# A list of ranks in place of due times, raw weights in the home of low parts, and other first products in an attention and gated-MLP kernel

## The chip, the cores and the metric

The kernel runs on one core of one Trainium2 chip. The metric is the device time of one launch in microseconds. The core has a matrix engine (PE, with its weight loads shown apart as PEld), three elementwise engines (DVE, ACT, POOL) and a queue engine, SP, that issues the DMAs.

## The reference

Four batches, four heads, 1088 positions, head width 32. Attention uses a feature map of 8 x 8 products instead of a softmax. Its output x (1088 x 128 per batch) goes through a gated MLP whose gate mixes positions with a 1088 x 1088 matrix.

```
a = S1 x ; b = S2 x ; phi(x) = outer(a, b).reshape(64)          # for q and k
kv = sum_s phi(k) v ; z = sum_s phi(k)
x = (phi(q) kv) / (phi(q) z + 1e-6)                             # per batch 1088 x 128
h = relu(x @ w_in) ; u, v = h[..., :512], h[..., 512:]
v_n = (v - mean(v)) / sqrt(var(v) + 1e-6)
v_s = w_spatial @ v_n + b_spatial                               # mixes the positions
out = (u * v_s) @ w_out
```

## The kernel before

All large products are done in split precision. An operand is a rounded high part plus a low part (the difference), and a product is three matrix instructions: high x high, low x high, high x low (`mm3`, `high`, `low`). ACT makes a high part by a cast, DVE or POOL makes the low part by a subtraction.

The spatial matrix W is loaded transposed, in 9 row tiles of 128 (`kt` 0 to 8) and 3 column pieces of 424, 332 and 332 (`c` 0 to 2; the text calls piece c "placement" c). `load_w(kt, c)` loads one raw tile `wt<kt><c>` into one of seven `pl` buffers, casts it into `wTh` and subtracts into `wTl`. The raw buffer is free again when both are done. For the first two pieces the subtraction runs on DVE, for the third on POOL. `wTh` and `wTl` are whole arrays of 9 x 1152 columns. `w_in` and `w_out` arrive as 64-bit numbers and are converted in seven DVE or ACT steps each (`from_f64`, tiles `wi_x1`, `wi_x0`, `wo_x`).

Batch 0 has a form of its own. `attention0` computes the keys' features (`kab`, `kp`), sums them into `kv0`, then per group of 384 positions computes the queries' features, turns them (`tq`), divides (`nd`, `rec`, `x32`), turns back (`xt`) and splits x into `xh` and `xl`; `hidden_v` makes `vt`, its mean and variance (`st`, `mv`, `rs`, `nm`) and normalises it. `main` then issues for batch 0 the products with the high part of W for all four column blocks d (`sp0d0`, kt 0 to 8), after them the products with its low part, then the gates (`u`, `g`) and the output products (`po`). Batches 1 to 3 do the same work in `attention` and `main` while the batch before is still on PE.

Nothing is executed in program order. Each operation is registered with `op` (engine, cost in ns, reads, writes) and a planner, `Order.schedule`, runs a timeline: at each step it takes, for each engine, the operations that could start within a small slack of the earliest one, and of these the one with the lowest `due`; the engine that can start first goes. A due time is worked back from the last operations with the costs, then moved by a table of numbers by name, `LEADS`. For DMAs the planner assumes one stream at 0.38 KB per ns, with 1950 ns until the first byte counts and once 1900 ns extra. The result is one fixed order per engine; on the chip every engine executes its own list in order and waits on semaphores.

Before the first data are there PE multiplies zeros (`N_WARM` products of 128 x 128, tile `wps`), and up to 50 us the planner puts unread products of 64 columns (`Fill`, L471) into gaps of PE that it foresees.

Of the kernel before, what the change touches and what calls it, by code (L numbers as in the profile page):

```python
# [45 lines left out]
}  # L46
DR_BUFS = {"qd": 6}
# [59 lines left out]
class Whole:  # L107


    def __init__(self, k, tag, name, shape, dt=F32):  # L110
# [16 lines left out]
class Fill:


    def __init__(self, fn):  # L130
        self.fn = fn


class Order:


# [73 lines left out]
    def schedule(self):  # L210
        ops = self.ops
        for o in reversed(ops):
            eng, cost, _ = o.alts[0]
            own = max(cost - self.OV[eng], 20) if eng != "PE" else cost + 165
            if eng == "SP":
                own = cost + 2000 + o.kb / 0.39
            own *= o.stretch
            dues = [s.due - own - self.LAT.get((eng, s.eng), 35) for s in o.succ]
            if o.due is not None:
                dues.append(o.due)  # L220
# [1175 lines left out]
```

## Time and profile before

| what | us |
|---|---|
| median of the three runs | 333.25 |
| the three runs | 327.79, 333.25, 333.78 |
| the profiled execution's own time | 326.74 |
| its span, first to last instruction | 325.0 |

The span is 1.74 us shorter than the time of the same execution. In the views, a line such as L978 is a line of the kernel, "sp<-wTl,vh" says what is written from which operands, and x8 how many instructions a row merges. Times are counted from the start of the span. Matrix instructions are pipelined: the duration of one is longer than the step from one to the next, so the text works with steps.

### The profile page before, as it was taken

The numbers are of one execution on the slowest core, as the hardware profiler recorded it, in microseconds if no ns is written. First come the engines' busy times: TensorE is split into PE (matmuls) and PEld (weight loads), VectorE is DVE, ScalarE is ACT, GpSimd is POOL, SyncE is SP. The second block draws the span as 40 slices with busy tenths as digits, with TensorE's granted clock in tenths as the row PEclk, the third lists the DMA queues.
The fourth block names the chain that finished last, engine by engine and source line by source line (L and its number), as shares of the span: only waits on it lengthen the run. The fifth ranks groups of instructions, "written<-read, shape, count | busy, mean of one in ns | idle before, by whom it ended". The sixth has DMA issues, their size and how long they took to land.

```text
span 325.0 us, 6726 instructions
## 1 busy us (share of the span) xinstructions
PE 318.4 (98%) x2580; PEld 303.7 (93%) x2580; DVE 228.6 (70%) x513; ACT 166.1 (51%) x390; POOL 64.6 (20%) x81
## 2 busy tenths in 40 slices
PE   8899999999999999999999999999999999999995
PEld 7787999899999899999899999999999999999995
DVE  4799997646699973789986558897235697429382
ACT  2498667435774634566536457562314465416050
POOL 1000002486101026320103802150001321103000
PEclk9999999999999999999999999999999999999999
DMA  7832168854020274001034206001000321000001
GB/s 216 288 105 87 54 173 272 266 172 131 3 69 20 83 239 162 1 5 45 21 117 137 63 30 185 2 0 37 8 0 2 105 86 42 0 3 0 2 1 69
DMA packets 21548, 26.82 MB, mean 83 GB/s; under 512 B 2828, under 2 KB 21260, under 8 KB 21516
## 3 DMA queue, kind: packets, MB, share of 16 engines
q1 hardware_dynamic: 21516, 26.39, 26.2%
q8 instruction: 20, 0.33, 0.4%
q14 instruction: 12, 0.10, 0.1%
HBM read 23.31 MB, written 3.06 MB: 81 GB/s over the span
## 4 chain that ended last, share of the span: by engine, by line
PE 81%; DVE 8%; DMA 5%; ACT 3%; SPq 2%; issue 1%; ACTq 0%
PE sp L969 16%; PE sp L971 14%; PE sp L978 14%; PE sd L1203 4%; PE sp L1203 3%; PE sd L444 3%; PE sd L445 3%; PE sd L446 3%; PE pu L444 2%; PE po L445 2%; PE po L444 2%; DMA pl<-in_wT 2%; PE po L446 2%; PE sp L980 2%; PE pu L445 2%; PE pu L446 2%
## 5 line engine op out<-in xcount | busy, mean ns | idle before, releaser
L969 PE MATMUL sp<-wTh,vh 128*128 128x332 f32 (+1 forms) x350 | 114.8, 328 | 0.0
L971 PE MATMUL sp<-wTh,vl 128*128 128x332 f32 (+1 forms) x304 | 98.9, 325 | 0.0
L978 PE MATMUL sp<-wTl,vh 128*128 128x332 f32 (+1 forms) x304 | 97.0, 325 | 0.0
L969 PEld LDWEIGHTS sp<-wTh,vh 128*128 128x128 f32 x350 | 65.8, 188 | 2.2 <-issue 1.0
L971 PEld LDWEIGHTS sp<-wTh,vl 128*128 128x128 f32 x304 | 57.1, 188 | 0.6
L978 PEld LDWEIGHTS sp<-wTl,vh 128*128 128x128 f32 x304 | 57.1, 188 | 0.2
L454 DVE TENSOR_TENSOR g<-u,g 128x332 fp32r<-128x332 f32 (+1 forms) x41 | 24.3, 593 | 18.1 <-PE po L445 11.6
L523 ACT CAST g<-u 128x332 fp32r<-128x332 f32 (+1 forms) x41 | 19.8, 490 | 31.9 <-DVE u L1006 21.6
L1006 DVE TENSOR_TENSOR u<-sp,u 128x332 f32<-128x332 f32 (+1 forms) x43 | 22.3, 520 | 19.1 <-PE sp L980 12.6
L779 DVE RECIPROCAL c<-c 128x384 f32<-128x384 f32 (+1 forms) x9 | 21.8, 2419 | 16.0 <-ACT c L777 16.0
L961 ACT ACTIVATE u<-pu 128x332 f32<-128x332 f32 (+1 forms) x44 | 20.6, 469 | 22.0 <-PE pu L446 17.7
L882 ACT CAST vh<-vt 128x384 fp32r<-128x384 f32 x36 | 17.3, 511 | 20.6 <-DVE vt L841 11.6
L805 DVE BATCH_NORM_STATS2 st<-vt 128x6 f32<-128x512 f32 x36 | 24.0, 684 | 2.2 <-ACT vt L803 2.0
L748 POOL TENSOR_TENSOR pl<-pl,pl 128x384 f32<-128x384 f32 (+1 forms) x18 | 17.9, 1004 | 37.4 <-DMA pl<-qd 37.3
L457 POOL TENSOR_TENSOR r<-pl,r 128x384 fp32r<-128x384 f32 (+1 forms) x18 | 17.7, 988 | 36.8 <-ACT r L523 36.8
L803 ACT ACTIVATE vt<-sd 128x512 f32<-128x512 f32 x36 | 21.3, 603 | 7.1 <-PE sd L446 6.3
L884 DVE TENSOR_TENSOR vl<-vt,vh 128x384 fp32r<-128x384 f32 (+1 forms) x36 | 17.8, 505 | 5.3 <-ACT vh L882 5.2
L570 POOL TENSOR_TENSOR wTl<-pl,wTh 128x332 fp32r<-128x332 f32 (+1 forms) x9 | 8.2, 935 | 55.5 <-ACT wTh L567 52.6
L444 PE MATMUL pu<-xh,wih 128*128 128x332 f32 (+1 forms) x48 | 16.5, 344 | 0.4 <-ACT kp L961 0.2
L841 DVE TENSOR_SCALAR vt<-vt,mv,sm 128x512 f32<-128x512 f32 x33 | 16.7, 556 | 0.0
L567 ACT CAST wTh<-pl 128x332 fp32r<-128x332 f32 (+1 forms) x27 | 12.7, 499 | 7.1 <-DMA pl<-in_wT 6.9
L446 PE MATMUL pu<-xh,wil 128*128 128x332 f32 (+1 forms) x48 | 15.8, 329 | 0.0
(279 smaller groups left out, 641.6 us busy)
## 6 DMA issues: line engine op xcount, KB each, us to landing
pl<-in_wT SPq DMA_DIRECT2D x34, 166.0 KB
v<-in_vA SPq DMA_DIRECT2D x12, 198.0 KB
kt<-in_kT SPq DMA_DIRECT2D x12, 192.0 KB
pl<-qd SPq DMA_DIRECT2D x12, 192.0 KB
pl<-qd SPq DMA_DIRECT2D x24, 96.0 KB
pl<-in_wT SPq DMA_DIRECT2D x9, 212.0 KB
c<-in_qT SPq DMA_DIRECT2D x9, 192.0 KB
out<-u SPq DMA_DIRECT2D x6, 166.0 KB
```

The costliest lines, as they stand in the source:

```text
L444: nc.tensor.matmul(o, ah, bh, start=start, stop=False)
L445: nc.tensor.matmul(o, ah, bl, start=False, stop=False)
L446: nc.tensor.matmul(o, al, bh, start=False, stop=stop)
L454: return lambda: nc.vector.tensor_tensor(out=o(), in0=a(), in1=bb(), op=ALU.subtract)
L779: op("DVE", 135 + 6.3 * n, lambda x32=x32, n=n: nc.vector.reciprocal(out=x32[:, :n], in_=x32[:, :n]), w=[x32])
L803: op("ACT", c_act(512, True), lambda pv=pv, t=t: nc.scalar.activation(vt[:, t], pv.ap, AF.Relu), r=[pv], w=[(vt, t)])
L805: op("DVE", 690, lambda stats=stats, t=t: nc.vector.bn_stats(out=stats.ap, in_=vt[:, t]), r=[(vt, t)], w=[stats])
L969: nc.tensor.matmul(sp[:, :cw], vh[:, kt], wTh[:, kt, cs], start=(kt == begin), stop=False)
L971: nc.tensor.matmul(sp[:, :cw], vl[:, kt], wTh[:, kt, cs], start=False, stop=False)
L978: nc.tensor.matmul(sp[:, :cw], vh[:, kt], wTl[:, kt, cs], start=False, stop=False)
L1006: op("DVE", c_dve(cw), lambda: nc.vector.tensor_tensor(out=u.ap, in0=sp[:, :cw], in1=u.ap, op=ALU.mult), r=[sp], w=[u], lead=LEAD[1])
L1203: nc.tensor.matmul(x[:, :cw], p, q, start=i == 0 and n == 0, stop=end and i == 3 and n == 2)
```

## The change

Five things are changed.

- The raw tiles of the first piece of W (kt 0 to 7) no longer use the `pl` buffers. The array `wTl` is cut into `wTl<kt>` (448 columns, piece 0) and `wl<kt>` (704 columns, pieces 1 and 2) at the same places in memory, and raw `wt<kt>0` is loaded into the home of `wl<kt>`, which is written for good only later, by the low parts of pieces 1 and 2.
- PE starts with 5 products of zeros in place of 8, and then issues 28 unread products of 32 x 32 columns at four positions of the array.
- Due times and `LEADS` go. `due` is the place of the operation in a list of 1806 names, `ORDER`; the planner and its slacks stay. (`FIRST` still sets a due time, which is then overwritten by the rank.)
- The planner's DMA model is slower: 0.265 KB per ns in place of 0.38, first byte after 1500 ns, once 500 ns extra. Some PE costs, the switch between 4-byte and rounded products (`TURN`) and the size given for `w_in` are raised.
- Loads get earliest times: 7 us for piece 0 of W, 13 us for pieces 1 and 2; those of batch 1 go from 35 to 24 us.

The computation is the same.

```diff
-N_WARM = 8
+N_WARM = 5
+N_SMALL = 28
...
+SB_BUFS.update((f"wl{kt}", 1) for kt in range(NK))
...
-    (0, "wTh", "wTl", "xh", "xl", "g", "c", "r", "b32"),
+    (0, "wTh", *(f"{x}{kt}" for kt in range(NK) for x in ("wTl", "wl")), f"wTl{NK}", "xh", "xl", "g", "c", "r", "b32"),
...
-FIRST = ()
-AFTER = (0, 35.0, 0, 0)
+FIRST = ("s_raw", "kt00", "kt01", "kt02", "v00", "v01", "v02", "qt00", "ident_sb", "mask_sb", "wi_raw1", "qt01")
+AFTER = (0, 24.0, 0, 0)
+AFTER_W = (7.0, 13.0, 13.0)
...
+ORDER = """
+kt00:1 z9:1 eps:2 z9:2 s_raw:1 eps:1 v92:1 wps:1 v93:1 v00:1 wps:2 v90:1 v91:1 wps:3 kt01:1 wps:4
+qt00:1 wps:5 kt02:1 wps:6 wi_raw1:1 sk:1 sk:2 b32:1 sk:3 sk:4 ident_sb:1 sk:5 sk:6 v01:1 sk:7 v02:1
+kab00:1 kab01:1 qt01:1 ka00:1 kp00:1 ka01:1 mask_sb:1 wt80:1 kp01:1 kab02:1 kv0:1 ka02:1 kp02:1 qab00:1 qa00:1 qp00:1
+wt50:1 wi_x1:1 qt02:1 tq00:1 bh:1 wi_x1:2 tq01:1 wi_raw0:1 qpT00:1 bl:1 kv0:2 wi_x1:3 qpT01:1 wt20:1 wi_x1:4 wt40:1
+kv0:3 wi_x1:5 wTl:11 qab01:1 kd0:1 wi_x1:6 wt00:1 nd00:1 qa01:1 wTh:9 wt10:1 qp01:1 wt01:1 wTh:6 wi_x1:7 tq10:1
+wt11:1 tq11:1 rec0:1 wTl:9 wih:1 qab02:1 rec0:2 wTl:6 qa02:1 x320:1 qpT10:1 qpT11:1 qp02:1 xt0:1 nd01:1 wt30:1
+wi_x0:1 wil:1 xh0:1 wt70:1 wi_x0:2 wTh:3 tq20:1 xl0:1 wt60:1 tq21:1 wTh:5 rec1:1 wi_x0:3 pv000:1 wt21:1 rec1:2
+wi_x0:4 wTh:1 wTl:10 pv001:1 x321:1 vt00:1 wt31:1 wi_x0:5 qpT20:1 xt1:1 st000:1 wt41:1 qpT21:1 pv002:1 xh0:2 wi_x0:6
+wt51:1 vt00:2 nd02:1 xl0:2 wTh:11 wo_raw:1 st001:1 vt00:3 wTh:10 wi_x0:7 wt61:1 pv010:1 wTh:8 mv00:2 rec2:1 wih:2
+st002:1 pv011:1 wTh:7 rec2:2 mv00:1 mv00:3 x322:1 qt10:1 qt11:1 vt01:1 qt12:1 wTl:7 vt01:2 xt2:1 wil:2 sd00:1
+pv012:1 wTh:12 xh0:3 rs00:1 st010:1 wTh:4 pu000:1 xl0:3 vt01:3 t100:1 wTh:2 st011:1 pv020:1 u000:1 t100:2 st012:1
+pv021:1 wTh:13 vt02:1 rs00:2 mv01:1 pu010:1 nm00:1 mv01:3 mv01:2 vt02:2 vt00:4 pv022:1 u010:1 wTl:8 vh00:1 pab10:1
+vt00:5 vt02:3 pu020:1 st020:1 vl00:1 abT10:1 sd01:1 pab11:1 vt00:6 qd10:1 pab12:1 rs01:1 wTl:3 qd10:2 sp000:1 abT11:1
+u020:1 t101:1 wTl:2 sp010:1 qd11:1 vh00:2 pu030:1 t101:2 wTl:1 vh00:3 qd11:2 sp030:1 rs01:2 vl00:2 wTh:15 sp020:1
+wTh:16 nm01:1 st021:1 vl00:3 sp030:2 vt01:4 sp000:2 st022:1 sp010:2 vt01:5 sp020:2 wTl:13 sp020:3 vh00:4 mv02:3 mv02:1
+wt71:1 mv02:2 sp010:3 vt01:6 vh00:5 sp030:3 vl00:4 sd02:1 sp000:3 vh00:6 rs02:1 vl00:5 sp020:4 wo_x:1 sp030:4 t102:1
+abT12:1 vl00:6 sp010:4 wTh:14 qd12:1 sp000:4 t102:2 wo_x:2 wTh:17 sp010:5 qd12:2 rs02:2 wTl:12 sp020:5 nm02:1 wo_x:3
...
+""".split()
...
-TURN = 125
+TURN = 150
...
+RATE, SLOW_AT, SLOW_BY, LATENCY = 0.265, 4000, 500, 1500
...
-            o.due = round((min(dues) if dues else 1e9) - o.lead)
+        rank = {name: n for n, name in enumerate(ORDER)}
+        for o in ops:
+            o.due = rank[o.name]
...
-                dma = max(dma, s + cost + 1950) + o.kb / (0.38 if o.kb > 0 else -0.12)
-
-                if dma > 5000 and not slow:
-                    slow, dma = True, dma + 1900
+                dma = max(dma, s + cost + LATENCY) + o.kb / (RATE if o.kb > 0 else -0.12)
+
+                if dma > SLOW_AT and not slow:
+                    slow, dma = True, dma + SLOW_BY
...
+    def small():
+        for i in range(N_SMALL):
+            q = 32 * (i % 4)
+            nc.tensor.matmul(wps[q:q + 32, :32], z9[:, q:q + 32], z9[:, :32], start=True, stop=True, tile_position=(0, q))
+
+    op("PE", 1000, f4=True, fn=small, r=[z9], w=[wps], due=0)
...
-    wTl = tl(None, "wTl", [P, NS, ROW], F32R)
+    wl_first = [tl(None, f"wTl{kt}", [P, WIDE], F32R) for kt in range(NK)]
+    wl_last = tl(None, f"wTl{NK}", [P, ROW], F32R)
+    wl_rest = {}
+
+    def w_lo(kt, c, n=P):
+        at, cw = AT[c], PIECES[c][1]
+        if kt == NK:
+            return wl_last[:n, at:at + cw]
+        return wl_first[kt][:n, :cw] if c == 0 else wl_rest[kt][:n, at - WIDE:at - WIDE + cw]
...
-        raw = tl("pl", f"wt{kt}{c}", [P, cw])
-        load(raw, lambda: raw[:, :cw], wT[kt * P:(kt + 1) * P, c0:c0 + cw], cw // 2)
+        raw = tl("pl" if c or kt == NK else f"wl{kt}", f"wt{kt}{c}", [P, cw])
+        load(raw, lambda: raw[:, :cw], wT[kt * P:(kt + 1) * P, c0:c0 + cw], cw // 2, after=AFTER_W[c])
...
-                op("PE", 410, f4=True, fn=lambda g=g, f=f: part(g, f), r=[f, vs[g]], w=[kv])
+                op("PE", 520, f4=True, fn=lambda g=g, f=f: part(g, f), r=[f, vs[g]], w=[kv])
```

In the list `wTl:1` to `wTl:9` are the low parts of piece 0 for kt 0 to 8, `wTl:10` and `wTl:11` the two DMAs of the bias, `wTl:12` to `wTl:20` the low parts of piece 1; `wTh:n` are the casts in the same manner.

## Rows read from the trace of the kernel before

**Rows 1.** The page, part 1: engine, busy us, share of the span, instructions.
```profile
PE 318.4 (98%) x2580; PEld 303.7 (93%) x2580; DVE 228.6 (70%) x513; ACT 166.1 (51%) x390; POOL 64.6 (20%) x81
```

**Rows 2.** The longest waits of PE after its start: who for whom, us in total, times, longest.
```profile
PE pu L630 <- issue: 0.9, 1, 0.9
PE po L445 <- DVE xh L454: 0.4, 1, 0.4
```

**Rows 3.** Stretches: length, PE, PEld, DVE, ACT, POOL (instructions), granted clock, DMA share, GB/s.
```profile
0.00:4.00 4.00, 2.67 (x12) 2.67 (x13) 0.87 (x6) 1.49 (x2) 1.22 (x8) 1.00 0.43 111
...
10.00:14.00 4.00, 3.02 (x118) 2.46 (x118) 2.50 (x7) 1.41 (x4) 0.00 (x0) 1.00 0.81 274
14.00:20.00 6.00, 6.00 (x61) 5.68 (x60) 5.91 (x13) 5.27 (x13) 0.00 (x0) 1.00 0.55 181
...
28.00:36.00 8.00, 7.78 (x41) 7.08 (x40) 8.00 (x26) 7.19 (x16) 0.00 (x0) 1.00 0.00 0
...
66.00:320.00 254.00, 254.00 (x1987) 245.17 (x1987) 173.11 (x382) 124.24 (x293) 56.75 (x66) 1.00 0.18 56
```

**Rows 4.** PE in order of time, first part: start, busy, line, operation, count, idle before.
```profile
4.91 0.53 PE L471 MATMUL po<-u 128*128 128x64 f32 x2
5.37 1.06 PE L593 MATMUL sd<-sk,kt 128*64 128x64 f32 x24
6.35 1.10 PE L471 MATMUL po<-u 128*128 128x64 f32 x8
7.41 0.57 PE L593 MATMUL sd<-sk,kt 128*64 128x64 f32 x12
7.90 0.63 PE L630 MATMUL pu<-v,kp 128*32 128x33 f32 x48
...
8.96 1.33 PE L471 MATMUL po<-u 128*128 128x64 f32 x10
10.41 1.15 PE L630 MATMUL pu<-v,kp 128*32 128x33 f32 x89
12.42 0.27 PE L630 MATMUL pu<-v,kp 128*32 128x33 f32 x7 [0.86 <-issue]
...
13.97 0.56 PE L471 MATMUL po<-u 128*128 128x64 f32 x4
14.37 1.67 PE L693 MATMUL sp<-u,c 128*128 128x66 f32 x12
...
17.12 0.88 PE L471 MATMUL po<-u 128*128 128x64 f32 x6
17.84 0.50 PE L707 MATMUL sp<-u,c 128*128 128x128 f32 x3
...
19.77 0.47 PE L444 MATMUL sd<-wih,xh 128*128 128x512 f32 x1
...
28.11 0.55 PE L471 MATMUL po<-u 128*128 128x64 f32 x4
28.88 0.46 PE L444 MATMUL pu<-xh,wih 128*128 128x424 f32 x1 [0.22 <-ACT kp L961]
```

**Rows 5.** The chain that ended last, at 4 us: start, us, what.
```profile
4.02 6.35 DMA v<-in_vA
```

**Rows 6.** Weight loads of the first unread products and of the fills: ns min/median/max, first and last start.
```profile
L467 PEld LDWEIGHTS sd<-u x16: 288/333/333, 1.3 to 4.5; 128*128 128x128 f32 x16
...
L471 PEld LDWEIGHTS po<-u x34: 186/192/333, 4.7 to 28.3; 128*128 128x128 f32 x34
```

**Rows 7.** SP in order of time.
```profile
10.39 4.06 SPq L451 DMA_DIRECT2D pl<-in_wT x7
...
37.92 1.90 SPq L451 DMA_DIRECT2D pl<-in_wT x3
```

**Rows 8.** DVE: low parts of W's first piece, and the last low part of v.
```profile
42.58 0.69 DVE L913 TENSOR_TENSOR vl<-vt,vh 128x512 fp32r<-128x512 f32 x1
43.19 2.12 DVE L570 TENSOR_TENSOR wTl<-pl,wTh 64x424 fp32r<-64x424 f32 x4
```

More of the change, by code (lines that the diff above doesn't have):

```diff
@@ new lines @@
+wih:6 u301:1 x20:3 wil:6 x20:4 s320:1 x20:5 sp320:8 x20:6 p70:1 e10:2 p70:2 u301:2 p70:3 x30:1 x30:2
+p70:4 ss0:2 x30:3 ss2:2 pu302:1 s120:2 p12:1 u302:1 x30:4 wih:7 sp320:9 wil:7 p12:2 s120:3 pu311:1 u320:2
+vh31:7 x30:5 vl31:6 gh320:1 p12:3 x30:6 s121:2 p12:4 s121:1 x40:1 gl320:1 gh301:1 e12:1 x40:2 ss1:2 x30:7
+u311:1 p52:1 ss3:2 e10:3 po30:3 s121:3 u302:2 x40:3 s121:4 gl301:1 gh302:1 x40:4 wih:8 pu312:1 wil:8 x40:5
+u312:1 p52:2 s121:5 x40:6 s121:6 p52:3 ss0:3 u311:2 p52:4 vh31:8 ss2:3 ob30:1 pu321:1 vl31:7 e52:1 po31:1
@@ new lines @@
+s321:1 s321:2 ss1:3 p62:1 gl302:1 gh311:1 x60:1 ss3:3 x22:1 u321:1 x60:2 x22:2 x60:3 x22:3 u312:2 po32:1
+p62:2 gl311:1 gh312:1 x22:4 x22:5 x32:1 x22:6 x32:2 u321:2 x32:3 p72:1 x32:4 p72:2 x32:5 p62:3 x32:6
+p62:4 p72:3 e12:2 p72:4 x32:7 pu322:1 e12:3 x42:1 u322:1 po31:2 u322:2 pu331:1 gl312:1 gh321:1 x42:2 u331:1
+x42:3 x62:1 po32:2 x62:2 pu332:1 gl321:1 gh322:1 x42:4 x62:3 u332:1 po31:3 u332:2 x42:5 pu330:1 gl322:1 x42:6
+sp330:1 u330:1 u331:2 sp330:2 gh331:1 sp330:3 gl331:1 gh332:1 sp330:4 gl332:1 sp330:5 sp330:6 sp330:7 sp330:8 sp330:9 po31:4
@@ L68 @@
+u330:3 po32:3 u330:2 ob31:1 po32:4 out:10 pl0:1 ob32:1 pl212:1 out:11 ob30:2 ob30:3 out:12 out:13
+""".split()
 LEAD = (6500, 3700)
@@ L123 @@
 class Op:
-    __slots__ = ("n", "name", "eng", "fn", "occ", "dur", "deps", "succ", "due", "left", "ready", "first", "tiles", "start", "end", "chosen", "alts", "kb", "rw", "stretch", "sh", "after", "lead", "f4")
+    __slots__ = ("n", "name", "eng", "fn", "occ", "dur", "deps", "succ", "due", "left", "ready", "first", "tiles", "start", "end", "chosen", "alts", "kb", "rw", "stretch", "sh", "after", "f4")
 class Fill:
@@ L146, in tile, with op @@
         return T(self, tag, name, shape, dt)
-    def op(self, eng, cost, fn, r=(), w=(), due=None, kb=0, alts=(), sh=False, kind=None, after=0.0, lead=0.0, f4=False):
+    def op(self, eng, cost, fn, r=(), w=(), due=None, kb=0, alts=(), sh=False, kind=None, after=0.0, lead=0.0, f4=False, name=None):
         o = Op()
@@ L151, in op @@
         o.alts = ((eng, cost, fn), *alts)
-        name = next(((x[0] if isinstance(x, tuple) else x).name for x in w), "out")
+        name = name or next(((x[0] if isinstance(x, tuple) else x).name for x in w), "out")
         self.named[name] = self.named.get(name, 0) + 1
@@ L158, in op @@
             assert o.alts, kind
-        o.stretch, o.sh, o.after, o.lead = self.stretch, sh, after * 1e3, lead + sum(LEADS.get(x, 0) for x in (*self.part, o.name))
+        o.stretch, o.sh, o.after = self.stretch, sh, after * 1e3
         deps = {}
@@ L211, in schedule @@
         ops = self.ops
[L212 to L220, printed above, removed]
-            o.due = round((min(dues) if dues else 1e9) - o.lead)
+        rank = {name: n for n, name in enumerate(ORDER)}
+        for o in ops:
+            o.due = rank[o.name]
         free = {"PE": 1300.0, "ACT": 1080.0, "DVE": 830.0, "POOL": 700.0, "SP": 740.0}
@@ L449, in load @@
         if t.name in FIRST:
-            kw["due"] = FIRST.index(t.name) - 1e4
+            kw["due"] = FIRST.index(t.name) * 2e4 - 1e7
         op("SP", 470, lambda: nc.sync.dma_start(out=ap(), in_=src), w=[w or t], kb=kb, **kw)
@@ L542, in tile_kernel, with w_lo_key @@
     wTh = tl(None, "wTh", [P, NS, ROW], F32R)
-    wTl = tl(None, "wTl", [P, NS, ROW], F32R)
+    wl_first = [tl(None, f"wTl{kt}", [P, WIDE], F32R) for kt in range(NK)]
[6 more added lines that the diff above has]
+        return wl_first[kt][:n, :cw] if c == 0 else wl_rest[kt][:n, at - WIDE:at - WIDE + cw]
+    def w_lo_key(kt, c):
+        if kt == NK:
+            return wl_last, (kt, c)
+        if c and kt not in wl_rest:
+            wl_rest[kt] = tl(f"wl{kt}", f"wl{kt}", [P, ROW - WIDE], F32R)
+        return (wl_rest[kt] if c else wl_first[kt]), (kt, c)
     wih = tl(None, "wih", [P, DFF], F32R)
@@ L550, in load_wi @@
         sl = slice(j * 512, j * 512 + 512)
-        load(raw, lambda: raw[:, :1024].bitcast(U32), w_in[:, sl].bitcast(U32), 524)
+        load(raw, lambda: raw[:, :1024].bitcast(U32), w_in[:, sl].bitcast(U32), 640)
         from_f64(x, raw, 512)
@@ L562, in load_w @@
         cs = slice(AT[c], AT[c] + cw)
-        raw = tl("pl", f"wt{kt}{c}", [P, cw])
-        load(raw, lambda: raw[:, :cw], wT[kt * P:(kt + 1) * P, c0:c0 + cw], cw // 2)
+        raw = tl("pl" if c or kt == NK else f"wl{kt}", f"wt{kt}{c}", [P, cw])
+        load(raw, lambda: raw[:, :cw], wT[kt * P:(kt + 1) * P, c0:c0 + cw], cw // 2, after=AFTER_W[c])
         n = 64 if kt == NS - 1 else P
         op("ACT", c_act(cw), lambda: nc.scalar.copy(out=wTh[:, kt, cs], in_=raw[:, :cw]), r=[raw], w=[(wTh, (kt, c))])
+        lo = w_lo_key(kt, c)
         def low(eng):
-            return lambda: eng.tensor_tensor(out=wTl[:n, kt, cs], in0=raw[:n, :cw], in1=wTh[:n, kt, cs].bitcast(F32), op=ALU.subtract)
-        op("POOL", c_pool(cw), low(nc.gpsimd), r=[raw, (wTh, (kt, c))], w=[(wTl, (kt, c))], alts=[("DVE", c_dve(cw), low(nc.vector))], sh=True, kind=f"W{c}")
+            return lambda: eng.tensor_tensor(out=w_lo(kt, c, n), in0=raw[:n, :cw], in1=wTh[:n, kt, cs].bitcast(F32), op=ALU.subtract)
+        op("POOL", c_pool(cw), low(nc.gpsimd), r=[raw, (wTh, (kt, c))], w=[lo], alts=[("DVE", c_dve(cw), low(nc.vector))], sh=True, kind=f"W{c}", name="wTl")
     def load_bias():
@@ L581, in load_bias @@
                 "SP", 470,
[L582 to L583 removed]
+                lambda n=n, t=t: nc.sync.dma_start(out=wl_last[64 + n:65 + n].bitcast(F32).rearrange("p (a c) -> p a c", c=16), in_=t.ap.bitcast(F32)),
+                r=[t], w=[(wl_last, ("bias", n))], kb=4, name="wTl",
             )
@@ L644, in keys @@
         fs = [features(b, g, at[g][0], "k", at[g][1]) for g in range(3)]
-        op("PE", 1230, f4=True, fn=lambda: [part(g, fs[g]) for g in range(3)], r=[*fs, *vs], w=[kv])
+        op("PE", 1700, f4=True, fn=lambda: [part(g, fs[g]) for g in range(3)], r=[*fs, *vs], w=[kv])
         return kv
@@ L977, in low @@
             if kt < NK:
-                nc.tensor.matmul(sp[:, :cw], vh[:, kt], wTl[:, kt, cs], start=False, stop=False)
+                nc.tensor.matmul(sp[:, :cw], vh[:, kt], w_lo(kt, c), start=False, stop=False)
             else:
-                nc.tensor.matmul(sp[:, :cw], vx[:66], wTl[:66, kt, cs], start=False, stop=True)
+                nc.tensor.matmul(sp[:, :cw], vx[:66], w_lo(kt, c, 66), start=False, stop=True)
         def spatial(d, c, sp, kt, parts=(high, low), begin=0):
@@ L992, in spatial @@
             if low in parts:
-                r += [(wTl, (kt, wc)) for wc in wcs] + ([(wTl, ("bias", 0)), (wTl, ("bias", 1)), vx] if kt == NK else [])
+                r += [w_lo_key(kt, wc) for wc in wcs] + ([(wl_last, ("bias", 0)), (wl_last, ("bias", 1)), vx] if kt == NK else [])
             def f():
```

92 lines of the change are left out of this document (87 added, 5 removed).

## Prediction

> **What bounds the kernel now.** The shares come first. PE is busy for 318.4 of 325.0 us [rows 1], so an edit is worth something only where PE afterwards has less to do or waits less. Busy is a weak measure here, as products that nobody reads count in it. Next I read the waits of PE: after its start the longest are 0.9 and 0.4 us [rows 2]. The table by stretch says where they can lie: from 66 to 320 us PE is busy for all of its 254.00 us, at a granted clock of 1.00 [rows 3]. Whatever the new order does there moves work that PE has to do anyway. So the gain has to come from the first 66 us, and there from unread products and waits.
>
> The order in time of PE's first 29 us shows these [rows 4]. From 1.3 to 4.9 us it multiplies zeros. The first real product starts at 5.37. Fills then take 6.35 to 7.41 (1.06 us), 8.96 to 10.41 (1.45), 13.97 to 14.37 (0.40), 17.12 to 17.84 (0.72) and, with a wait of 0.22, 28.11 to 28.88 (0.77). In the sums of the keys' features there is a hole of 0.86 us that ends at 12.42, for which the profile knows no releaser. DVE is the second thing to see: it is busy for 5.91 of 6.00 us from 14 to 20 and for 8.00 of 8.00 from 28 to 36 [rows 3]. The short stage before the dense products is therefore DVE's, and PE fills what DVE leaves.
>
> **The change, part by part.** The base is the profiled execution: span 325.0, time 326.74, thus 1.74 us around the span. The middle of the three runs shown is 333.25, 6.5 us above this execution; the lowest, 327.79, is near it. No row says what the upper two spent more.
>
> First products. Three of eight products of zeros go. Each is two instructions; the 16 begin at 1.3 and the first fill follows at 4.91 [rows 4, 6], so one takes 3.6 / 16 = 0.225 us: 6 x 0.225 = 1.35 us less. 28 small products, 56 instructions, are added. The nearest row is the sum of the keys' features with 32-column weights: 48 instructions in 0.63 us at 7.90 [rows 4], 0.013 us each, so 0.74 us; at half that speed 1.5 us. PE is then through with them at 1.3 + 2.25 + 0.74 to 1.5, thus 4.3 to 5.05 us, in place of 4.91. Both lie ahead of 5.37, when the first feature product has its data. The cover is this arrival: it waits for the conversion of S on DVE, whose raw tile is the second DMA in the old and in the new order. On the path: 0. Without the cover it would cost at most 1.5 - 1.35 = 0.15 us.
>
> The fills from 6.35 to 10.41, 2.5 us together. What ends the first no row here says; the second ends at 10.41 when the last v tile, on its way since 4.02, has landed [rows 5]. In the new list v01 and v02 still stand behind the first half of w_in, 512 KB, with some 70 KB of small loads more ahead of them. I take 0, the value of the second fill, between +0.25 (70 KB at the 274 GB/s of 10 to 14 us [rows 3]) and -2.5 (both gone).
>
> The hole of 0.86 us. The small products add 112 instructions with their weight loads and the three dropped ones take 12 away, so the place where PE's stream stopped will be reached some 100 instructions earlier. Nothing shows if the hole is bound to the place or to the moment. I take 0; from -0.86 (gone) to +0.86 (a second one).
>
> Fills and waits after 12.42. 0.40 + 0.72 + 0.77 of fills and 0.4 of a wait for a gate [rows 2, 4] make 2.3 us, and with the hole 3.2. This is all that a better order can get back, as everything behind is full. To get it PE must have real work sooner, which DVE has to release, and DVE is full with the same operations in both kernels. What the list can do is take the ones first for which PE waits. I take two thirds of 2.3 us, 1.5 us, because the order of the division and of the means in the list is not tied to due times worked back from the end, and no more, because DVE has no idle time there to give. Ends: 0 and 3.2.
>
> Raw W in the home of the low parts. The bytes, the casts and the subtractions stay, and so do the places of the parts in memory (448 + 704 = 1152 columns). What goes is the wait of SP for a `pl` buffer: before, seven W tiles leave at 10.39 and the next three only at 37.92 [rows 7], after DVE has subtracted, while the DMA engines carry 0 GB/s from 28 to 36 us [rows 3]. That wait is not on PE's path: PE's products with these tiles come late, and PE has no wait there. Moving SP's issues costs elsewhere: `wt80` and `wt50`, 424 KB, now stand ahead of the second half of w_in and the last q tile; at 274 GB/s that is 1.5 us later. The DMA engines carry only 181 GB/s from 14 to 20 us against 274 in the stretch before [rows 3], so they have room to catch up, and DVE works on the first half meanwhile; I count 0, at most +1.5. The loads of batch 1, and of W's second piece that are pulled forward, fall into the empty stretch.
>
> The list for the rest, and the costs. From 66 us on there is no wait to remove, and none is added if the plan holds: 0, from -0.5 (fewer switches between kinds of products) to +2 (a gate that PE meets too early, five times the 0.4 of rows 2).
>
> Sum: 326.74 - 1.5 = 325.2 us, span 323.5.
>
> **The rivals.** [...]
>
> *Low parts of W push batch 0 (slower).* DVE is full; in the old order four of the nine low parts of W's first piece come after the last low part of v [rows 8], so at most five lie ahead of it. In the list seven of nine and three of the second piece rank ahead of the last two: five more than before, at 2.12 / 4 = 0.53 us each, 2.7 us later for the last v. It decides from the point where PE has no product left that can start; then the time is 326.7 + 2.7 = 329.4. Against it: each such part releases four products of PE as well.
>
> *The gaps only move.* DVE sets the stage and its sum is unchanged: 326.7. For it speaks DVE's 8.00 of 8.00.
>
> **How the numbers follow.** Forecast 325.2 (322.5 to 326.5): 0.45. Clock later, or a middle run in the upper place for a reason not shown: 330.6, up to 333.5, 0.25. Low parts ahead: 329.4, 0.12. Gaps only move: 326.7, 0.13. Something else, mostly worse: 0.05. The lower end adds up the bounds below zero: 326.74 less 3.2 of gaps with the hole, 2.5 of early fills and 0.5 of switches is 320.5. The upper end is 330.6 with the 2 us and the 0.86 of the unknown costs, 333.5. Range 320.5 to 333.5. About 2% is what a measurement of this kernel can tell from no change, given runs that lie 1.8% apart. Against the profiled execution 2% would be 320.2, which no case reaches; against the printed middle, 326.6, which the forecast does. I give the second reading a little over half: faster 0.30. Slower needs 333.3 or more against the low runs: 0.09. Same 0.61.
>
> **What would show it.** After 5 us weight loads of 190 ns; no fill after 12.5 us longer than 0.4; PE full from about 28 us; the last product some 1.5 us earlier. [...] I am wrong as a whole if PE waits after 66 us.

## The result, and the profile after

The changed kernel took 332.48 us (median of four: 331.74 to 332.99), the kernel before beside it 327.8: ratio 1.014, 95% interval 1.010 to 1.018. Measured again with the last experiment it was 1.023 (1.012 to 1.034). The forecast was a gain of 1.5 us; the change costs 4.7. Ratios here and below leave out executions over 1.5% above the fastest of the same kernel; for the kernel before these are the ones of 332.9 us and up, which beside the experiments show a mean granted clock of 0.979 or less where the others show 0.994 or more, and without them its medians there are 326.7 to 327.3.

The profiled execution of after took 332.94 us, span 331.1, mean granted clock 0.993. The waits of PE after its start come first, as in [rows 2] (who for whom, us in total, times, longest):

```profile
PE sp L1107 <- POOL vl L1049: 4.4, 1, 4.4
...
PE pu L555 <- ACT u L1097: 1.0, 1, 1.0
PE pu L766 <- issue: 0.7, 1, 0.7
PE sd L729 <- DMA kt<-in_kT: 0.6, 1, 0.6
```

One wait is new and long: PE waits 4.4 us for POOL, for a low part of v. In order of time, PE's first 29 us and then the place of that wait, against [rows 4]:

```profile
1.32 2.50 PE L578 MATMUL sd<-u 128*128 128x128 f32 x10 [1.32 <-DVE u L574]
3.75 0.98 PE L583 MATMUL sd<-u 128*32 128x32 f32 x56
4.66 0.69 PE L590 MATMUL po<-u 128*128 128x64 f32 x2
5.28 0.98 PE L729 MATMUL sd<-sk,kt 128*64 128x64 f32 x24
...
12.84 0.75 PE L766 MATMUL pu<-v,kp 128*32 128x33 f32 x63 [0.73 <-issue]
...
16.75 1.33 PE L590 MATMUL po<-u 128*128 128x64 f32 x10
...
44.53 0.35 PE L1107 MATMUL sp<-wTh,vl 128*128 128x424 f32 x1
44.72 0.35 PE L1105 MATMUL sp<-wTh,vh 128*128 128x424 f32 x1
49.46 0.46 PE L1107 MATMUL sp<-wTh,vl 128*128 128x424 f32 x1 [4.39 <-POOL vl L1049]
...
50.05 0.56 PE L1107 MATMUL sp<-wTh,vl 128*128 128x424 f32 x1
50.40 0.56 PE L1105 MATMUL po<-wTh,vh 128*128 128x424 f32 x1
```

After the wait one product follows the other in 0.35 us (50.05 to 50.40), ahead of it in 0.19 (44.53 to 44.72). The stretches (columns as in [rows 3]) say why:

```profile
44.00:49.00 5.00, 1.07 (x6) 0.72 (x4) 4.96 (x11) 2.71 (x7) 5.00 (x1) 1.00 0.71 189
49.00:50.00 1.00, 0.54 (x2) 0.53 (x3) 0.96 (x1) 0.48 (x2) 0.92 (x2) 0.91 0.89 262
50.00:53.00 3.00, 3.00 (x10) 2.80 (x10) 0.00 (x0) 0.98 (x2) 2.92 (x4) 0.50 0.57 184
53.00:54.00 1.00, 1.00 (x6) 0.95 (x5) 0.00 (x0) 0.00 (x0) 1.00 (x2) 0.88 0.67 178
...
66.00:320.00 254.00, 252.69 (x1991) 244.14 (x1990) 175.23 (x380) 124.51 (x294) 53.23 (x63) 1.00 0.19 57
```

PE stood still from 45.1 to 49.5, then the granted clock was 0.50 from 50 to 53 us and 0.88 in the next: the 13 products from 49.46 to 53.63 take 1.7 us more than at 0.19 each, lost beside the 4.4. From 66 us on PE now lacks 1.31 us of 254; before it lacked none.

What POOL and DVE did there (start, us, engine, line, operation):

```profile
35.33 1.30 POOL L1049 TENSOR_TENSOR vl<-vt,vh 128x512 fp32r<-128x512 f32 x1 [32.99 <-ACT vh L1046]
43.28 6.13 POOL L1049 TENSOR_TENSOR vl<-vt,vh 128x512 fp32r<-128x512 f32 x1 [6.65 <-DVE vl L1049]
49.49 1.61 POOL L1058 TENSOR_TENSOR vh<-vt,vh 64x512 fp32r<-64x512 f32 x1
```

```profile
42.55 0.69 DVE L1049 TENSOR_TENSOR vl<-vt,vh 128x512 fp32r<-128x512 f32 x1
43.16 0.92 DVE L706 TENSOR_TENSOR wl<-pl,wTh 128x332 fp32r<-128x332 f32 x2
43.99 0.60 DVE L706 TENSOR_TENSOR wTl<-wl,wTh 128x424 fp32r<-128x424 f32 x1
...
47.18 0.50 DVE L706 TENSOR_TENSOR wl<-pl,wTh 128x332 fp32r<-128x332 f32 x1
47.60 0.69 DVE L637 SCALAR_TENSOR_TENSOR v<-kt,v 128x512 f32<-128x512 uint32 x1
48.32 1.64 DVE L638 TENSOR_TENSOR v<-v 128x512 f32<-128x512 f32 x1
```

The same subtraction takes 0.69 us on DVE and 1.30 on POOL (at 35.33) beside statistics with one input (DVE L941, st<-vt, 1.28 us for two). At 43.28 it takes 6.13, while eleven operations pass on DVE, mostly low parts of W. It ends 1.1 us after the first pause in DVE's stream (48.29 to 48.32: until then each operation had begun before the former ended), and the operation after the pause takes 1.64 instead of 0.69. In [rows 8] all this was on DVE: the last v at 42.58, the low parts of W behind it.

An account of PE in the two profiled executions (326.74 and 332.94 us), from its timeline (each instruction to the start of the next; idle, fills and the first unread products taken out):

| PE, us | before | after |
|---|---|---|
| idle | 2.86 | 8.76 |
| fills | 4.64 | 4.76 |
| first unread products | 3.58 | 3.34 |
| the products that are needed | 310.48 | 310.89 |
| end of the last product | 321.56 | 327.75 |

The needed products contain the 1.7 us of the low clock; without it they take 1.3 us less than before, for a reason that was not traced. So between these two executions 6.2 us are lost net: 4.4 and 1.7 at the place above, 1.0 in a wait at 250.38, and smaller ones, against 1.3 won.

### The profile page after: what moved, and what is told of

It reads as the page before. It is cut to its first block, busy times and chain, and to the rows that moved or that the text cites. A ratio compares the mean times of both kernels' runs of the same rounds, so it can differ in the third digit from the quotient of the medians.

```text
span 331.1 us, 6815 instructions
## 1 busy us (share of the span) xinstructions
PE 318.8 (96%) x2630; PEld 303.8 (92%) x2630; DVE 227.2 (69%) x509; ACT 166.0 (50%) x391; POOL 72.3 (22%) x84
## 4 chain that ended last, share of the span: by engine, by line
PE 82%; ACT 7%; DVE 4%; POOL 2%; issue 2%; DMA 1%; SPq 1%; ACTq 0%; POOLq 0%
PE sp L1105 16%; PE sp L1114 14%; PE sp L1107 14%; PE sd L1339 4%; PE sp L1339 3%; PE sd L555 3%; PE sd L557 3%; PE sd L556 3%; PE po L556 2%; PE sp L1116 2%; PE po L555 2%; PE pu L555 2%; PE po L557 2%; PE pu L556 2%; PE pu L557 2%; PE sd L729 2%
## 5 line engine op out<-in xcount | busy, mean ns | idle before, releaser
L1114 PE MATMUL sp<-wl,vh 128*128 128x332 f32 x192 | 59.8, 311 | 0.0
L1114 PE MATMUL sp<-wTl,vh 128*128 128x424 f32 x112 | 38.4, 354 | 0.0
L1114 PEld LDWEIGHTS sp<-wl,vh 128*128 128x128 f32 x192 | 36.1, 188 | 0.0
L941 DVE BATCH_NORM_STATS2 st<-vt 128x6 f32<-128x512 f32 x36 | 24.6, 688 | 12.5 <-ACT vt L939 12.3
L565 DVE TENSOR_TENSOR g<-u,g 128x332 fp32r<-128x332 f32 (+1 forms) x41 | 23.7, 578 | 5.5 <-PE po L556 3.7
L884 POOL TENSOR_TENSOR pl<-pl,pl 128x384 f32<-128x384 f32 (+1 forms) x18 | 18.0, 1004 | 38.1 <-DMA pl<-qd 22.7
L1114 PEld LDWEIGHTS sp<-wTl,vh 128*128 128x128 f32 x112 | 21.2, 190 | 0.3
L1020 DVE TENSOR_TENSOR vl<-vt,vh 128x384 fp32r<-128x384 f32 (+1 forms) x36 | 18.5, 530 | 2.8 <-ACT vh L1018 2.5
L736 DVE TENSOR_TENSOR kp<-ka,sd 128x768 f32<-128x768 f32 x15 | 14.0, 949 | 3.3 <-ACT ka L734 3.2
```

The lines of the kernel that those rows point to most:

```text
L565: return lambda: nc.vector.tensor_tensor(out=o(), in0=a(), in1=bb(), op=ALU.subtract)
L941: op("DVE", 690, lambda stats=stats, t=t: nc.vector.bn_stats(out=stats.ap, in_=vt[:, t]), r=[(vt, t)], w=[stats])
L1114: nc.tensor.matmul(sp[:, :cw], vh[:, kt], w_lo(kt, c), start=False, stop=False)
```

## The experiments

Theory A: DVE and POOL shut each other out, nothing else was lost. Theory B came after the first runs: the list puts low parts of W ahead of those of v on DVE, so v is late whichever engine makes it. Rivals: clock and first products, loads and home, the planned DMA rate. Every edit makes the planner place all operations anew, so the waits elsewhere move too.

**a_one**, the low part of tile 7 back on DVE:

```
-FORCE = {..., 'vl0': ['DVE', 'POOL'], ...}
+FORCE = {..., 'vl0': ['DVE', 'POOL'], 'vl07': ['DVE'], ...}
-... kind="vl0")
+... kind="vl07" if kt == 7 else "vl0")
```

> The changed kernel with one placement turned back: the low part of v for key tile 7 is subtracted on DVE instead of POOL; the list, the new homes, the lower DMA rate and the first products stay. [...] Rival that the first products or the clock's rise cost the time: stays at 332. [...] Rival that POOL was merely given too much to do: the next POOL operation in its list becomes late, 329 to 331.

332.71 us, 1.016 (1.012 to 1.021). A miss: what was expected was 326 to 327.5 us, with no wait for POOL and a granted clock of 1.00 behind it. The wait only changed its owner. The next operation in POOL's list, the ninth row tile, is now the one that stands:

```profile
43.07 5.95 POOL L1058 TENSOR_TENSOR vh<-vt,vh 64x512 fp32r<-64x512 f32 x1 [7.43 <-ACT vh L1046]
```

PE waits 2.2 us for it after 1.04 us of fills. The last rival of its expectation comes nearest, though the cause is not POOL's load: it had been idle for 7.43 us.

**a_alldve**, all of v of batch 0 on DVE (`'vl0': ['DVE']`):

> The changed kernel with all eight low parts of v of the first batch, and the ninth of 64 rows, on DVE as in the kernel before. Theory: the same as with one placement turned back, 326 to 328; two or three operations of 0.7 us more on DVE, which is full there, can cost up to 1 us of it as waits on DVE. If the placement on POOL is a help apart from this one operation, this run is slower than the one with a single placement turned back by over 1 us. Rivals (clock, loads): 332.

331.21, 1.012 (1.010 to 1.014). The granted clock stays at 1.00, and still 3.0 us are missing in the same place: fills of 1.95 (one at 38.1) and a wait of 1.05. POOL now begins the third piece of W at 46.77 (before: 54.95), and DVE pays:

```profile
46.77 8.33 POOL L706 TENSOR_TENSOR wl<-pl,wTh 128x332 fp32r<-128x332 f32 x6 [44.42 <-ACT wTh L702]
```

```profile
45.57 0.69 DVE L1049 TENSOR_TENSOR vl<-vt,vh 128x512 fp32r<-128x512 f32 x1
...
47.95 1.27 DVE L1058 TENSOR_TENSOR vh<-vt,vh 64x512 fp32r<-64x512 f32 x1
49.25 1.09 DVE L706 TENSOR_TENSOR wl<-pl,wTh 128x332 fp32r<-128x332 f32 x1
```

```profile
44.80 1.22 PE L590 MATMUL po<-u 128*128 128x64 f32 x10
...
47.76 0.56 PE L590 MATMUL po<-u 128*128 128x64 f32 x4
49.36 0.43 PE L1105 MATMUL sp<-wTh,vh 128*128 128x424 f32 x1 [1.05 <-DVE vh L1058]
```

The last v ends at 46.26, 3.0 us later than the 43.27 of [rows 8]. This gave theory B.

**b_pool7**, the kernel before with tile 7 planted on POOL (`'vl07': ['POOL']`):

> The kernel before with one placement planted: the low part of v for key tile 7 on POOL. Theory: if DVE has a stream of subtractions without a pause when POOL starts, the operation takes 3 to 6 us instead of 0.7 and PE waits 2 to 5 us for it, with the clock down after that: 329 to 333. If DVE has pauses there, it takes 1.3 to 1.9 us, as other subtractions of this shape on POOL, and the time is 327 to 328. Rivals (clock, loads, queue of the new kernel): no change to the kernel before, and POOL's operation of some 1.3 us wherever it stands.

331.47, 1.010 (1.007 to 1.012). POOL's subtraction took 1.46 us, with a pause of DVE (0.03 us) 0.3 us after its start, and PE did not wait for it. The time was lost elsewhere, the most in waits of up to 1.3 us far behind (ending at 105.0 and 122.8 us): this edit costs 1% by planning everything anew. As a test of theory A it settles nothing.

**a_warm8**, eight products of zeros, no small ones:

> The changed kernel with the eight products of zeros of the kernel before and without the 28 small ones. Theory: within 0.7 us of the changed kernel, 332 to 333.5, the wait on POOL still there, since the start is hidden behind the arrival of the first data. Rival that the first products set the clock's rise: back towards 327 to 328, and weight loads of 192 ns earlier than in the changed kernel.

333.77 to 337.47, 1.026 (1.021 to 1.032); its one profiled execution can't be used (last section). Not faster, so the first products do not hold the 4.7 us. On a steadier base, **a_w2warm8** below, the question has its answer.

**a_w2dve**, all low parts of v and of W's third piece on DVE (`'vl0': ['DVE']`, `'W2': ['DVE']`):

> The changed kernel with all low parts of v of the first batch on DVE, and the nine low parts of W's third piece on DVE too, so that POOL computes nothing between 12 and about 58 us. Theory A (POOL and DVE slow each other; nothing else was lost): DVE's instructions between 47 and 52 us are back at 0.5 and 0.69 us, PE has neither wait nor fill from 38 to 50 us, 326.5 to 327.5, ratio about 1.00. Theory B (the list puts 10 to 14 low parts of W ahead of the last low part of v where the kernel before has 4, so the last v is late whichever engine makes it): 0.6 us less than the kernel with only v on DVE, the 2 us of fills between 38 and 48 us stay, ratio 1.008 to 1.011. Rival that the loads or the planned DMA rate are the cause: no change to the kernel with only v on DVE, 1.012.

329.69, 1.010 (1.008 to 1.012). Theory B's figure. POOL does nothing from 2.3 to 59.6 us, and PE still has fills of 0.37, 1.04 and 0.55 us and a wait of 0.48 between 37 and 48 us, so theory A alone does not hold.

**a_vfirst2** and **a_fix2** turn the order, with W's third piece on POOL and on DVE:

```
+LATER = [x for x in ORDER if x in {f"wTl:{n}" for n in (*range(1, 10), *range(12, 21))}]
+ORDER = [x for x in ORDER if x not in LATER]
+ORDER[ORDER.index("vh00:10") + 1:ORDER.index("vh00:10") + 1] = LATER
```

> The changed kernel with the low parts of v of the first batch on DVE, and in the list the low parts of W's first and second piece behind the last of v (they still go in between where nothing else is ready: 5 of them ahead of the last v instead of 14). The third piece stays on POOL. Theory B: the last v is done some 3 us earlier than with v on DVE alone (43 in place of 46.3 us), no fills and no PE wait on DVE or POOL between 38 and 50 us, though POOL's subtractions still take 1.3 us each and more: 1.0 us of wait at 249 us and 0.7 us of early fills stay, ratio 1.000 to 1.005. Theory A: PE still waits for what POOL and DVE hold up near 49 us, ratio 1.009 to 1.012.

> Both edits at once: low parts of v ahead of those of W, and the third piece of W on DVE. If both theories hold, each for its part, PE is full from 28 us on but for the wait of 1.0 us at 249 us: 326.5 to 327.5, ratio 0.998 to 1.003. If the list's order from 66 us on, the loads or the planned rate cost something as well, it stays above 1.006.

330.6, 1.012 (1.010 to 1.014), and 1.024 (1.017 to 1.030; four executions from 329.44, the profiled one, to 336.39). The local forecast held: no fill and no wait of PE from 30 to 50 us, last v at 43.39 and 41.99. The times missed: fills near 25 and 28 us grew by 1.1 us, and waits of 0.5 and 1.4 us stand near 95 and 109 us. For a_vfirst2 1.012 is theory A's figure, but without the wait near 49 us from which theory A had it. In the profiled executions what was won was given back where the planner moved other work.

**a_oldlist**, the changed code with the order of the kernel before as its list:

> The changed kernel's code with the order of the kernel before put in the place of its list: new home of raw W, early loads of W, small first products, the new DMA costs in the planner, and DVE's and POOL's work of the first 60 us in the old sequence. Theory B (the list is at fault, the other parts cost nothing): no fill and no wait between 30 and 55 us, 326 to 328, ratio 0.997 to 1.004. Rival that home, loads or the planned DMA rate cost the time: 1.008 to 1.015, with waits on DMA or with DVE behind it.

334.12, 1.019 (1.015 to 1.024). A miss: PE has only 0.6 us of fills from 30 to 56 us, near what theory B wants, but a hole of 2.1 us at 12.96 and waits of 1.3 us at 97 and 223 us, one with the granted clock at 0.50 behind it. An order made for other costs isn't a good order here; home and loads are not cleared by this run.

**a_nopool**, **a_w2warm8** and **a_rate** stand on a_w2dve: later sums without POOL; the old first products; `RATE, SLOW_AT, SLOW_BY, LATENCY = 0.38, 5000, 1900, 1950`.

> The kernel with the low parts of v and W on DVE, and the sums and low parts of the later batches that the planner may give to either engine on DVE alone; POOL keeps 18 sums and 18 subtractions of the queries' and keys' features. Theory A: the waits of 1.0 us at 247 us and of 0.9 us at 195 us go, since nothing holds DVE's gate there: 1 to 2 us less than the kernel it is built on (ratio 1.010), thus 1.004 to 1.007. Rival that DVE becomes late by its own load (some 35 operations of 0.4 to 0.5 us more): waits on DVE of the same size, 1.010 or more.

> The kernel with the low parts of v and W on DVE, with the eight products of zeros of the kernel before and without the 28 small ones. Prediction on record: nothing on the path, within 0.5 us of the kernel it is built on (ratio 1.010). Rival that the first products decide when the clock rises: 1.5 us and more apart, with weight loads of 192 ns from another moment on.

> The kernel with the low parts of v and of W's third piece on DVE, planned with the DMA costs of the kernel before (rate 0.38, 1950 ns). If the lower planned rate costs time by itself, this is 1 us or more below the kernel it is built on (ratio 1.010); if it only moves places in the order, within 0.7 us of it.

a_nopool: 329.23, 1.008 (1.004 to 1.013); three of its ten executions lie 3.8 us above the others, none of a_w2warm8's ten and none of a_mix1's. The wait at 247 us is gone, as theory A says, that at 196 stays (0.95, no releaser); the gain is within the interval. a_w2warm8: 329.35, 1.006 (1.003 to 1.008), in microseconds 0.3 from its base: the first products are worth next to nothing where the clock rises at about 5 us in both profiled executions. a_rate: 332.54, 1.020 (1.013 to 1.028), slower; going back to the higher planned rate wins nothing with this list.

**a_late**, a_w2dve with raw W's second and third piece loaded later (`AFTER_W = (7.0, 37.5, 46.0)`):

> The kernel with the low parts of v and of W's third piece on DVE, with one more edit: the loads of W's second piece may start only from 37.5 us and those of the third from 46 us, about when the kernel before issues them; the list, the homes, the planned rate stay. If the early arrival of W lets DVE make low parts of W ahead of those of v, this takes back the fills between 37 and 48 us (1.95 us) and the wait of 0.48 us at 48 us: 1 to 2.4 us less than the kernel it is built on (ratio 1.010), thus 1.003 to 1.007. If the list's ranks alone do it, nothing changes there.

330.4, 1.014 (1.006 to 1.022). It missed its aim: 12 low parts of W still came ahead of the last v, since the planner takes what is ready, and the gap stayed. In its profiled execution (334.0 us, the others 329.8 to 330.9) the clock rose late, at 17.5 us, as told under a_order. Nothing follows about the loads.

**a_mix1** and **a_mix2**: a_nopool with the old first products and the order turned, for eleven low parts of W (`(4, 5, *range(12, 21))` in `LATER`) and for all eighteen:

> New homes and list, with the eight products of zeros of the kernel before, all low parts and the later sums on DVE, and in the list the second piece's low parts of W and two of the first behind the last of v (9 instead of 14 low parts of W ahead of it). Where the causes add up: without the wait of 1.0 us at 247 us and with one to two of the 2.4 us between 37 and 48 us given back, ratio 0.998 to 1.003. If new waits take their place again, 1.005 and more.

> The same with all low parts of W's first and second piece behind the last of v in the list (5 instead of 14 ahead of it). No fill and no wait between 30 and 50 us; if nothing else moves, 0.995 to 1.002. If the places of the other work move as in the earlier kernel with this order (waits of 0.6, 0.5 and 1.4 us at 54, 95 and 109 us), 1.004 to 1.008.

a_mix1: 327.51, 1.003 (1.0005 to 1.005), all but 0.3% is back. a_mix2: 332.08, 1.017 (1.014 to 1.019), a miss, with the waits near 54, 95 and 109 us of a_fix2 and a hole of 2.1 us at 129.7 without a releaser, behind which the granted clock is 0.50 for 3.4 us.

**a_order**, the changed kernel with the list's eleven entries moved and nothing else, and **after_again** on the same chip:

> The changed kernel with one edit to its list: the nine low parts of W's second piece and two of the first stand behind the low part of v's last tile; which engine makes each low part is left to the planner, as in the changed kernel. Theory B with A as its consequence: at most 9 low parts of W come ahead of the last v, the planner then keeps all but one low part of v on DVE by itself, PE's wait of 4.4 us and the 1.8 us at the lower clock go, 3.5 to 5 us less than the changed kernel, ratio to the kernel before 1.000 to 1.005. If POOL's share of the work is a cause of its own apart from the order, waits for it remain near 50 us and the ratio stays above 1.007.

> The changed kernel once more, on the same chip as the run beside it: ratio 1.010 to 1.018, PE's wait for POOL L1049 of some 4 us again, and the granted clock down after it.

a_order: 328.38 (326.77 to 332.36), 1.002 (0.997 to 1.006), by the median of all ten executions 1.003; after_again: 333.67 (332.93 to 337.23), 1.023 (1.012 to 1.034). All ten of a_order lie below all four of after_again. With v first the planner itself leaves one low part to POOL, where it disturbs nothing, and PE has no wait from 43 to 50 us; 0.6 us of its 7.00 are a fill at 46.35 (POOL in order of time; the stretch):

```profile
38.56 1.30 POOL L1053 TENSOR_TENSOR vl<-vt,vh 128x512 fp32r<-128x512 f32 x1 [36.22 <-ACT vh L1050]
53.23 6.42 POOL L710 TENSOR_TENSOR wl<-pl,wTh 128x332 fp32r<-128x332 f32 x6 [13.38 <-ACT wTh L706]
```

```profile
43.00:50.00 7.00, 7.00 (x40) 6.72 (x39) 6.94 (x18) 4.07 (x11) 0.00 (x0) 1.00 0.12 23
```

This profiled execution took 332.36 us and stands 3.2 us behind after at 20 us (its fills of 19.98 are those of 16.75 there); the ten executions lie at 326.8 to 328.6 (six) and 331.5 to 332.4 (four). PE's timeline shows where this one lost its time: fills of equal number take 1.97 and 2.40 us where after has 1.10 and 1.33, and the same six turns (L819) take 1.49 us at 13.35 and 0.82 at 18.73. The clock rose at about 18 us here, not at 5: the trace's record of the granted clock begins with 1.00 at 17.64 us in a_order and 17.54 in a_late, at 5.71 in before, 5.45 in after and 4.8 to 7.4 in the other kernels, and the 1.00 that the views print for the time ahead of it, as in [rows 3], is no reading. PE had been busy without a gap from 1.32 us on. No execution of the lower six was profiled.

```profile
6.76 1.97 PE L594 MATMUL po<-u 128*128 128x64 f32 x8
...
11.16 2.40 PE L594 MATMUL po<-u 128*128 128x64 f32 x10
13.35 1.49 PE L819 MATMUL po<-u,kp 128*128 128x128 f32 x6
...
18.73 0.82 PE L819 MATMUL po<-u,kp 128*128 128x128 f32 x6
```

In after_again POOL's operation took the same 6.13, with the same 4.4 us of PE's wait, and the granted clock fell earlier: it is 0.88 from 44 to 49 us and 0.50 from 49 to 53.

```profile
42.80 6.13 POOL L1049 TENSOR_TENSOR vl<-vt,vh 128x512 fp32r<-128x512 f32 x1 [6.66 <-DVE vl L1049]
```

**m_port** and **m_port2** measure the two engines alone; they compute nothing of the reference.

> A kernel of its own that computes nothing of the reference: POOL's subtraction of 128x512 with two inputs in SBUF, alone and beside streams of DVE without a pause: subtractions of two SBUF inputs of 332 columns, single-input multiplications of 512, subtractions with one input in PSUM, subtraction and multiplication by turns, subtractions of 512 and of 64 columns. Theory of a shared way into SBUF: alone about 1.3 us (as beside single inputs in the changed kernel), beside single inputs the same, beside an unbroken stream of two-input subtractions not done until the stream ends or nearly so (20 times 0.4 us, 8 us), and DVE not slowed until late. Rival that POOL was late for a semaphore: 1.3 us everywhere.

> A kernel of its own that computes nothing of the reference: one POOL subtraction of 128x512 that is released in the middle of an unbroken stream of DVE subtractions with two inputs in SBUF; first with DVE operations that wait for nothing, then with inputs that ACT wrote (a wait already fulfilled for each), then released just ahead of the stream. If DVE's stream keeps the way into SBUF once it runs, POOL's operation ends only with the stream or its first gap, 5 us and more; if the two engines take turns as in the first kernel of this kind, it ends after 1.3 to 1.6 us and one DVE operation takes 1.5 us instead of 0.49.

m_port, by line (ns min/median/max): DVE's operations with two SBUF inputs (L72, first row), with one in PSUM (second), single-input multiplications of 512 columns (L77), and POOL's subtraction (L80):

```profile
L72 DVE TENSOR_TENSOR o<-a,b x84: 209/492/1751, 12.6 to 78.4; 128x64 fp32r<-128x64 f32 x40, 128x332 fp32r<-128x332 f32 x30, 128x512 fp32r<-128x512 f32 x14
L72 DVE TENSOR_TENSOR o<-bank,b x20: 494/494/504, 36.5 to 44.3; 128x332 fp32r<-128x332 f32 x20
...
L77 DVE TENSOR_SCALAR o<-a x30: 414/418/1486, 24.3 to 54.4; 128x512 fp32r<-128x512 f32 x30
...
L80 POOL TENSOR_TENSOR po<-pa,pb x20: 1255/1300/1705, 7.1 to 72.6; 128x512 fp32r<-128x512 f32 x20
```

In m_port DVE is held up beside POOL, also with a single input (1.49 in place of 0.42 us), but not where its second input is in PSUM (at most 0.50 us). POOL is not the one that is held up for long: it never took over 1.71 us, and one DVE operation per POOL operation took some 1.1 us longer. m_port2 gave the same in the middle of a stream: POOL 1.37 to 1.45 us, then one DVE operation of 1.56 in place of 0.49. So the 6.13 us are not reproduced outside the kernel.

## Why the prediction was wrong, point by point

The measured time lies inside the stated range, but only because its upper end had been set for a clock that rises late; that is luck. The gap of PE from 30 to 56 us, waits and fills together, against how many low parts of W DVE had begun before the last v began and when that was done (profiled executions):

| kernel | low parts of W ahead of the last v | last v done | PE's gap |
|---|---|---|---|
| before | 4 | 43.27 | 0 |
| a_vfirst2 | 4 | 43.39 | 0 |
| a_fix2 | 4 | 41.99 | 0.61, at 53.0 for a gate on DVE |
| a_mix2 | 4 | 42.75 | 0.83, at 53.8 for a gate on DVE |
| a_oldlist | 7 | 45.69 | 0.59 |
| a_order | 8 | 47.30 (3.2 us late from the start) | 0.72 |
| a_mix1 | 9 | 44.44 | 0.36 |
| a_late | 12 | 49.39 (3.2 us late from the start) | 2.81 |
| a_w2dve | 14 | 45.58 | 2.44 |
| a_alldve | 14 | 46.26 | 3.00 |
| a_one | 14 | 45.21, ninth tile 49.02 | 3.26 |
| after | 11, and 18 at its end | 49.41 on POOL | 4.39 |

- *DVE is full with the same operations in both kernels*, and from it *fills and waits after 12.42: -1.5*. This step failed. DVE was as full, but of work in another order, and the planner gave three operations of it to POOL: tiles 2 and 7 of v and the ninth row tile. The prediction had no term for a product that waits on POOL. The fills and waits meant came to 2.16 us against 2.34; the gain forecast did not come, and 4.39 + 1.7 us were added behind them.
- *Low parts of W push batch 0*, the rival at 0.12. Its mechanism was the right one: the last v 3.0 us late where DVE makes it (a_alldve), for 2.7 forecast. That the two are so near is luck: the 2.7 counts five low parts more ahead of the last two v, and ahead of the last there were ten more (14 against 4). And it did not see that v would go to POOL and POOL would stand behind DVE. That the order decides is shown by a_order: one edit to the list takes 1.023 to 1.002, with home, loads, planned costs and first products of the changed kernel in place.
- *Clock later*, at 0.25: a granted clock that rises later behind the new first products. It is not what made after slow: in after the weight loads of 128x128 change level where [rows 6] has it,

```profile
L578 PEld LDWEIGHTS sd<-u x10: 289/333/334, 1.3 to 3.2; 128*128 128x128 f32 x10
```

```profile
L590 PEld LDWEIGHTS po<-u x34: 186/192/337, 4.7 to 27.9; 128*128 128x128 f32 x34
```

  and from 4.9 to 49.7 us none takes over 230 ns (from 50.05 to 52.88, at the granted clock of 0.50, they take 331). The clock fell only behind the wait of 4.4 us, which cost 1.7 us. But a late rise does occur: the record of the granted clock begins with 1.00 at 17.64 us in a_order and at 17.54 in a_late, and in these profiled executions that cost 3.2 us by 20 us. No run shows the 5.4 us by which the 330.6 of this case stands above the 325.2 of the forecast; what the runs showed in their place are these 3.2. With the small first products (a_nopool, a_order) seven of twenty executions are some 4 us longer than the rest, with eight products of zeros (a_w2warm8, a_mix1) none of twenty. That the small products make it likelier is the plain reading, not shown: the kernels differ in other edits too, and of the seven only one was profiled.
- *First products: 0.* Right for the path: the first real product starts at 5.28 (5.37 before), and a_w2warm8 is 0.3 us from its base. The 56 small ones took 0.91 us (3.75 to 4.66), within the 0.74 to 1.5 of the sum. Their other price may be the one just told.
- *Fills 6.35 to 10.41: 0*, with the hole. Fills, wait and hole from 6 to 13 us take 3.82 us against 3.37, by a wait of 0.6 for the third key tile, which had no term; the fills alone are unchanged (2.50).
- *The hole*: 0.73 against 0.86, and bound to a place. PE had started 221 products in both kernels, with the small ones counted; the last section says more.
- *Raw W in the home of low parts: 0.* In [rows 7] three tiles leave at 37.92, after the first seven; now the tiles in `pl` leave by 24 us,

```profile
13.75 0.90 SPq L562 DMA_DIRECT2D pl<-in_wT  x2
...
18.18 1.46 SPq L562 DMA_DIRECT2D pl<-in_wT  x3
23.52 0.50 SPq L562 DMA_DIRECT2D pl<-in_wT  x1
```

  and with that, low parts of W's second piece are ready for DVE between 36 and 43 us. With v first no cost of the home shows: a_order has it and is level with before, within its interval. With the list as it is a_late was to tell, and missed its aim.
- *From 66 us on: -0.5 to +2.* 1.3 us, inside. 1.0 of it stands at 250.38, where PE waits for ACT and ACT for DVE's L565, which takes 1.21 in place of 0.49 while POOL subtracts:

```profile
248.58 1.21 DVE L565 TENSOR_TENSOR g<-u,g 128x332 fp32r<-128x332 f32 x1
```

```profile
248.54 0.90 POOL L1176 TENSOR_TENSOR xh<-pl,kt 128x332 fp32r<-128x332 f32 x1 [1.32 <-PE pu L557]
```

  With POOL out (a_nopool) this wait is gone. By its own words the prediction was wrong as a whole if PE waits there.

The prediction had not looked at POOL. Beside the streams of m_port POOL's subtraction got its turn after the operation of DVE that ran and took at most 1.71 us; in after, at 43.28, it was passed by eleven operations and took 6.13. No run shows what POOL waited for there.

## What to carry to other kernels

A list that tells a full engine what to do first is a choice of what is late last: count, for the operation that the bound engine waits for, how many others now stand ahead of it, and price those. Where a planner may move work to another engine, its choice is part of the change; look at the order it makes, not only at the list. In this kernel an operation on POOL was late three times by the rest of DVE's stream (6.13, 6.13 and 5.95 us), though not in m_port (at most 1.71); until that is understood, nothing that PE waits for belongs on POOL beside such a stream.

## What was not expected of the hardware

- POOL's subtraction stood behind DVE in three executions (6.13, 6.13 and 5.95 us), each time until the first pause in DVE's stream, 4.8 to 5.0 us after its start, and ended 1.09 us after DVE's next start; in m_port and m_port2, whose streams have no such pause either, it got its turn after the operation that ran (at most 1.71 and 1.45 us). What makes the difference is not settled.
- The hole without a releaser near 12 us sits, in the nine profiled executions that have it, at a place in PE's instructions, not at a moment. Products started ahead of it, and where it ended:

```
before 221, 12.42    after 221, 12.84    a_w2dve 221, 11.66    a_vfirst2 221, 12.52
a_oldlist 222, 12.96    a_w2warm8 221, 12.47    b_pool7 221, 12.96
a_nopool 221, 12.05    a_mix1 221, 13.23
```

  Its length is 0.27 to 2.13 us. A block of 0.02 MB (16384 bytes in the trace) comes in on the queue for instructions just ahead of it (DMA view of after, 9 to 13 us), with the engines at 91% for other loads:

```profile
q1 hardware_dynamic: 761, 1.14, 91.1%
q8 instruction: 1, 0.02, 1.4%
```

  In these nine executions the hole ends 1.04 to 1.61 us after the block has landed; in the other eight profiled executions of this family at the usual speed, after_again among them, PE comes to the place 1.33 to 5.50 us after the block and has no hole. That PE waits for its instructions fits this, but no run changes the block alone.
- One execution of a_warm8 lasted 1098.63 us: the products with W's high part took 861 ns on average where after has 329, and from 100 to 1000 us PE does 2024 products, where after does 1991 in 254 us. The 1.00 printed for its clock is no reading, as its trace has no record of the granted clock at all. Nothing in the kernel explains it.
